# The third differences' product leaves the output bank by a ScalarE copy and an adding DMA of its own

## The chip, the cores and the metric

One core of a Trainium2 chip runs the kernel. The metric is the device time of one execution in microseconds (us). The engines are TensorE (PE in the profile, its weight loads PEld), VectorE (DVE), ScalarE (ACT) and GpSimd (POOL); SyncE (SP) only issues DMAs here.

## The reference

Block-causal attention over 4 x 8 heads, then a soft mixture of 8 experts over all 2304 tokens, then a gated layer. The edit concerns the middle part:

```python
x = attn_out.transpose(0, 2, 1, 3).reshape(B * S, H * D)   # 2304 x 512
logits = x @ w_gate; P = np.exp(logits - logits.max())
for _ in range(8):                                         # balance rows and columns
    P /= P.sum(1, keepdims=True) + 1e-09
    P /= P.sum(0, keepdims=True) + 1e-09
    P *= N / E
for e in range(E):                                         # E = 8, F = 1024, D = 512
    h = np.maximum(x @ w1[e], 0.0)
    out += P[:, e:e + 1] * (h @ w2[e])
...
return silu(out @ w_gate2) * (out @ w_val) @ w_out
```

## The kernel before

The hidden columns of the 8 experts are cut into 16 units of 512 (`NU`), two to an expert. The 2304 tokens stand as two halves of 1152, and a half is cut into five blocks: four of 256 tokens (two tiles of 128) and one of 128. A step (u, b) takes block b of both halves through unit u.

Both matrix products of a step are done as 2 x 2 block products with seven multiplications instead of eight: the operands are X11, X12, X22, the sums S1 and S2, and the differences S3 and S4. Each operand is held as two fp16 parts, and each multiplication is three fp16 matmuls. `products_in` makes the first product (banks `abc` in PSUM, drained at L541 to L561), `sums_out` and `operand` make the operands of the second one (L663 to L693), and `products_out` makes the second product (banks `m_o_b` and `m_o_ac`). TensorE alternates between the two: six matmuls of a `products_in` step, six of a `products_out` step, the latter some steps behind.

In `products_out` the bank `b` of a tile is a running sum: X11, then S2, S3 and X22 are added to it in PSUM, and after each of them `take` carries the half of the result that is then complete out of the bank. So S2's matmuls wait until X11's result has been taken, S3's until S2's, and X22's until S3's. For units 2 to 14 `take` scales a result by the token's routing weight into an SBUF buffer `ev` (from a shared pool, `places`), and a DMA that adds in flight puts it on the accumulator `acc`:

- the first half of the tokens: X11 and S2 fill one buffer, which is added after S2; S4 fills a second one, 512 wide, added after S4;
- the second half: S1's result is copied into the right half of a buffer, S3's result is added to it there by VectorE (L1418), X22's result goes into the left half, and the whole is added after X22.

All other results are taken by ScalarE (L1421). The adds are issued by GpSimd (L1414), one step after the result (`later(1, add)`). The last unit is added to `acc` by VectorE without a buffer.

The same engines do other work in this stage: the weights of the next unit are loaded (L359), reduced (L363), scaled and split (L173, L174) and combined (L292), and the weights of the last layer are converted from a 64-bit raw form (L446 to L458, loaded by L418 into a buffer that is there once). All engines run their instructions in the order of the program, which the Python loop sets.

Of the kernel before, what the change touches and what calls it, by code (L numbers as in the profile page):

```python
# [9 lines left out]
F32 = mybir.dt.float32  # L10
# [3 lines left out]
AF = mybir.ActivationFunctionType  # L14
ALU = mybir.AluOpType
# [9 lines left out]
X11, X12, S4, X22, S1, S2, S3 = range(7)  # L25
# [5 lines left out]
def attention_moe_glu_kernel(  # L31
# [21 lines left out]
    nc = tc.nc  # L53
    B, NPAIR, P, S = qT.shape
    D = 64
    DM = v.shape[2]
    E, _, FF = w1.shape
# [14 lines left out]
    blocks = [(c, min(TB, NH - c)) for c in range(0, NH, TB)]  # L72
# [147 lines left out]
    places = Places(0)  # L220
# [272 lines left out]
    due, load = {}, [0.0]  # L493

    def later(d, f):

        due.setdefault(clock[0] + d, []).append(f)
# [77 lines left out]
    def plain_out(jobs, b, bank, free, every=7, last=False):  # L575


        done = 0
        tiles = tiles_of(b)
        for t, i, ii in tiles:  # L580
            for n, (h, W, evac) in enumerate(jobs):
                p = bank(t * NI + i, n)
                for c in range(2):
                    for j, (r, k, sh, mh) in enumerate(
                        (r, k, sh, mh) for r in range(2) for k in range(2) for sh, mh in ((0, 0), (0, 1), (1, 0))
                    ):
                        nc.tensor.matmul(  # L587
                            p[:, c * TB : (c + 1) * TB],
                            h[t, r][:, sh, k, ii * P : (ii + 1) * P],
                            W[r, c][:, mh, k],  # L590
                            start=c == 0 and j == 0,
                            stop=True,
                            skip_group_check=True,
                        )
                        done += 1
                        if done % every == 0 and not (c == 1 and j == 11):
                            yield True
                if (t, i, ii) == tiles[-1] or (t == 0 and ii == blocks[b][1] // P - 1):
                    places.give(h[t, 0], h[t, 1])
                if last and (t, i, ii) == tiles[-1]:  # L600
                    places.give(*W.values())
                evac(t * NI + i, p)
                free(p)
                if done % every == 0 or n == len(jobs) - 1 and (t, i, ii) == tiles[-1]:
                    yield True
# [642 lines left out]
    with tc.manual_schedule():  # L1248
# [16 lines left out]
        def unweighted(u, dst):  # L1265


            def evac(t, p):
                if u == 0:
                    nc.scalar.activation(dst(t), p, AF.Copy, scale=units[0][2])  # L1270
                else:
                    nc.vector.scalar_tensor_tensor(dst(t), p, units[1][2], dst(t), op0=ALU.mult, op1=ALU.add)

            return evac
# [58 lines left out]
        acc = accp.tile([P, NT, DM], F32, tag="acc", name="acc")  # L1333
# [6 lines left out]
        def m(name):  # L1340
            tag = mfree.popleft()
            t = ps_m1.tile([P, DM], F32, tag=tag, name=f"m_{name}")
            mtag[id(t)] = (tag, t)
            return t
# [32 lines left out]
        def scale_acc():  # L1377

            x = unscaled.popleft()
            nc.scalar.activation(acc[:, x], acc[:, x], AF.Copy, scale=pr[:, x, 0:1])  # L1380

        def expert_out(u, b):
            h = hts.pop((u, b))
            if u < 2:
                f = unweighted(u, lambda t: acc[:, t])
                yield from plain_out([(h, units[u][1], f)], b, lambda t, n: m(f"{u}_{b}_{t}"), mdone, 7, b == NB - 1)
                return
            if b == 0:
                for _ in steps:
                    pass  # L1390
                bg.until((u, 1))
                pe = pes[u] = small.tile([P, NT], F32, tag="pe", name=f"pe_{u}")
                nc.vector.tensor_scalar(pe, pr[:, :, u * FU // FF], units[u][2], None, op0=ALU.mult)

            def take(i, t, cols, ps, what=None):
                if t is None:
                    while u == 2 and (i in unscaled or NI + i in unscaled):
                        scale_acc()
                    return
                x = t * NI + i  # L1400
                p = pes[u][:, x : x + 1]
                a = acc[:, x, cols]
                wide = cols.stop - cols.start > TB
                load[0] += 280 if wide else 165
                if u == NU - 1:
                    nc.vector.scalar_tensor_tensor(a, ps, p, a, op0=ALU.mult, op1=ALU.add)
                    return
                k = (i, t, what == S4)
                if k not in ev:
                    ev[k] = places.take(f"ev{u}_{b}_{x}_{what}", F32)  # L1410
                e = ev[k].rearrange("p a b -> p (a b)")

                def add(x=x, e=e, k=k):
                    nc.gpsimd.dma_start(acc[:, x], e, accum_op=ALU.add)  # L1414
                    places.give(ev.pop(k), left=8)

                if what == S3:
                    nc.vector.scalar_tensor_tensor(e[:, cols], ps, p, e[:, cols], op0=ALU.mult, op1=ALU.add)  # L1418
                else:
                    load[0] -= 280 if wide else 165  # L1420
                    nc.scalar.activation(e[:, cols], ps, AF.Copy, scale=p)  # L1421
                if what in (S2, S4, X22):
                    later(1, add)

            yield from products_out(f"o{u}_{b}", b, h, units[u][1], m, mdone, take, b == NB - 1)

        pes, ev = {}, {}
# [298 lines left out]
```

## Time and profile before

| | |
|---|---|
| median of 3 runs | 2119.81 us (2118.15 to 2122.05) |
| the profiled execution | 2121.61 us, span 2119.8 us |
| TensorE busy in the span | 1968.2 us (93%) |
| VectorE | 1685.4 us (80%) |
| ScalarE | 1335.6 us (63%) |
| GpSimd | 537.0 us (25%) |
| units 2 to 14 leave the banks | from 480 to 1632 us |

Busy time is the sum of the intervals in which an engine executes; the rest is idle, and the trace names for each idle interval what ended it. Matmuls overlap, so the mean time of one is longer than the step from one to the next.

### The profile page before, as it was taken

To read this page: it belongs to the slowest core of one execution; us is meant where nothing else is said; L and a number is where in the kernel's file an instruction comes from. 1 tells how busy PE (TensorE), PEld (TensorE's weight loads), DVE (VectorE), ACT (ScalarE), POOL (GpSimd) and SP (SyncE) were. 2 spreads that over 40 slices of the span, in tenths; PEclk is the share of its full clock that TensorE was granted. 3 is DMA by queue.
4 is the path that set the end of the run, shared out by engine and by line. 5 is a ranking of instruction groups with operands and counts; after the bars stand their busy time and mean duration, and the time that the engine had idled before them with its cause. 6 is when DMAs were issued, how large, how long until landed. Compare 5 with 4: busy or idle time off the path is not lost.

```text
span 2119.8 us, 47322 instructions
## 1 busy us (share of the span) xinstructions
PE 1968.2 (93%) x18378; PEld 1683.5 (79%) x18378; DVE 1685.4 (80%) x3739; ACT 1335.6 (63%) x2823; POOL 537.0 (25%) x808
## 2 busy tenths in 40 slices
PE   6789899799999999999999999999899988999998
PEld 3456676698888888888888888888788877888887
DVE  7887775678888888888888788888887877666766
ACT  5666666348776777767777677777665566543442
POOL 4534444002222222222222222222222132100000
PEclk8889999899999999999999999999999999999999
DMA  5333331315666656766566675666757100201111
GB/s 152 110 99 100 88 108 39 120 31 105 123 163 121 155 111 119 162 127 155 110 122 156 128 160 120 144 131 125 165 120 175 31 16 1 84 23 29 53 41 51
DMA packets 152705, 221.07 MB, mean 104 GB/s; under 512 B 15392, under 2 KB 69664, under 8 KB 152480
## 3 DMA queue, kind: packets, MB, share of 16 engines
q0 software_dynamic: 50544, 92.04, 25.5%
q1 hardware_dynamic: 101936, 126.01, 19.5%
q8 instruction: 144, 2.36, 0.5%
q14 instruction: 81, 0.66, 0.1%
HBM read 90.98 MB, written 24.38 MB: 54 GB/s over the span
## 4 chain that ended last, share of the span: by engine, by line
PE 51%; DVE 21%; issue 4%; ACT 3%; DMA 2%; POOL 0%; SPq 0%; DVEq 0%; ACTq 0%; POOLq 0%
PE abc_m_b L524 10%; PE m_o_b L632 10%; PE m_o_ac L632 7%; PE abc_m_c L524 5%; PE abc_m_a L524 3%; PE m_go_b L632 3%; PE abc_g_b L524 3%; DVE m_t L691 3%; PE abc_v_b L524 3%; DVE m_h L183 2%; PE m_go_ac L632 2%; DVE w L174 2%; DVE m_h L667 2%; PE abc_g_c L524 1%; PE abc_v_c L524 1%
## 5 line engine op out<-in xcount | busy, mean ns | idle before, releaser
L524 PEld LDWEIGHTS <-w 128*128 128x128 f16 x6720 | 614.3, 99 | 126.2 <-issue 58.3
L632 PEld LDWEIGHTS <-m_h 128*128 128x128 f16 x5292 | 516.4, 98 | 84.2 <-issue 20.2
L1414 POOL DMA_DIRECT2D acc<-ev x351 | 302.8, 874 | 945.9 <-ACT ev L1421 758.5
L524 PE MATMUL abc_m_b<-xs,w 128*128 128x256 f16 (+1 forms) x3840 | 483.1, 266 | 38.2 <-DVE m_t L546 33.6
L632 PE MATMUL m_o_b<-w,m_h 128*128 128x256 f16 x3024 | 408.2, 274 | 19.1 <-ACT ev L1421 16.7
L632 PE MATMUL m_o_ac<-w,m_h 128*128 128x256 f16 x2268 | 310.8, 273 | 0.0
L524 PE MATMUL abc_m_c<-xs,w 128*128 128x256 f16 (+1 forms) x1920 | 231.6, 264 | 7.0 <-ACT m_r L760 5.1
L1421 ACT ACTIVATE ev<-m_o_b,pe 128x256 f32<-128x256 f32 x351 | 160.6, 473 | 66.6 <-PE m_o_b L632 60.3
L663 ACT ACTIVATE m_h<-m_t 128x512 f16<-128x512 f32 (+1 forms) x210 | 122.3, 583 | 85.0 <-DVE m_t L561 60.1
L1421 ACT ACTIVATE ev<-m_o_ac,pe 128x256 f32<-128x256 f32 (+1 forms) x234 | 134.3, 578 | 52.4 <-PE m_o_ac L632 51.4
L173 ACT ACTIVATE w<-wr,ws 128x512 f16<-128x512 f32 x210 | 150.0, 719 | 22.7 <-DVE ws L376 19.4
L174 DVE SCALAR_TENSOR_TENSOR w<-wr,ws,w 128x512 f16<-128x512 f32 x210 | 156.4, 746 | 7.6 <-ACT w L173 7.6
L670 ACT CAST m_h<-m_t 128x512 f16<-128x512 f32 (+1 forms) x210 | 121.6, 579 | 50.7 <-DVE m_t L691 49.8
L183 DVE TENSOR_TENSOR m_h<-m_t,m_h 128x512 f16<-128x512 f32 (+1 forms) x210 | 132.9, 634 | 6.1 <-ACT m_h L670 5.8
L667 DVE SCALAR_TENSOR_TENSOR m_h<-m_t,m_h 128x512 f16<-128x512 f32 (+1 forms) x210 | 130.2, 633 | 1.6 <-ACT m_h L663 1.6
L524 PEld LDWEIGHTS <-gg_w 128*128 128x128 f16 x1260 | 113.5, 98 | 20.9 <-issue 9.5
L632 PEld LDWEIGHTS <-g_h 128*128 128x128 f16 x1134 | 111.7, 99 | 19.5 <-issue 5.4
L524 PEld LDWEIGHTS <-gv_w 128*128 128x128 f16 x1260 | 113.6, 98 | 13.2 <-issue 1.7
L983 POOL TENSOR_SCALAR e<-e,r 128x64 f32<-128x64 f32 (+2 forms) x144 | 78.1, 548 | 168.5 <-DVE r L978 106.9
L524 PE MATMUL abc_m_a<-xs,w 128*128 128x256 f16 (+1 forms) x960 | 118.8, 264 | 0.0
L587 PEld LDWEIGHTS <-m_h 128*128 128x128 f16 x864 | 83.7, 99 | 16.9 <-issue 7.0
L363 DVE TENSOR_REDUCE wmx<-wr 128x1 f32<-128x512 f32 x128 | 86.2, 679 | 10.3 <-DMA wr<-in_w_dram 9.9
(315 smaller groups left out, 3310.9 us busy)
## 6 DMA issues: line engine op xcount, KB each, us to landing
acc<-ev POOLq DMA_DIRECT2D x351, 256.0 KB, 3.9
wr<-in_w_dram SPq DMA_DIRECT2D x128, 256.0 KB, 4.9
st<-hl SPq DMA_DIRECT2D x48, 144.0 KB, 3.6
raw_g<-in_w_gate_dram SPq DMA_DIRECT2D x12, 512.0 KB, 4.5
raw_v<-in_w_val_dram SPq DMA_DIRECT2D x12, 512.0 KB, 4.5
raw_o<-in_w_out_dram SPq DMA_DIRECT2D x12, 512.0 KB, 4.9
scr_g<-gg SPq DMA_DIRECT2D x21, 256.0 KB, 3.1
scr_v<-gv SPq DMA_DIRECT2D x21, 256.0 KB, 3.1
```

Of the source, the lines that this page charges most:

```text
L173: nc.scalar.activation(hi, src, AF.Copy, scale=s)
L174: return lambda: nc.vector.scalar_tensor_tensor(lo, src, s, hi, op0=ALU.mult, op1=ALU.subtract)
L183: nc.vector.tensor_sub(lo, src, hi)
L363: nc.vector.tensor_reduce(g["mx"][:, k : k + 1], g["b"][k // 2][k % 2], axis=AX.XY, op=ALU.max, apply_absolute_value=True)
L524: nc.tensor.matmul(ps[:, f], W[o][:, sh, k, f * P : (f + 1) * P], xs[:, o, mh, k, c0 : c0 + n], start=x not in begun, stop=True, skip_grou ...
L587: nc.tensor.matmul(p[:, c * TB : (c + 1) * TB], h[t, r][:, sh, k, ii * P : (ii + 1) * P], W[r, c][:, mh, k], start=c == 0 and j == 0, stop ...
L632: nc.tensor.matmul(ps, h[o][:, sh, k, ii * P : (ii + 1) * P], W[o][:, mh, k], start=o in (X11, X12) and k == 0 and j == 0, stop=True, skip ...
L663: nc.scalar.activation(hi, src, AF.Relu)
L667: nc.vector.scalar_tensor_tensor(lo, src, 0.0, hi, op0=ALU.max, op1=ALU.subtract)
L670: nc.scalar.copy(hi, src)
L1414: nc.gpsimd.dma_start(acc[:, x], e, accum_op=ALU.add)
L1421: nc.scalar.activation(e[:, cols], ps, AF.Copy, scale=p)
```

## The change

For S3, `take` no longer adds into the tile's buffer. ScalarE writes the scaled result into a new buffer that both tiles of the block share, and when the block's last tile is in it, an adding DMA of its own puts it on the right half of the second half's rows of `acc`. The tile's old buffer then holds S1 and X22 only, and is added after X22 as before.

```diff
@@ take, for units 2 to 14 @@
+                if what == S3:
+                    k = (b, S3)
+                    ii, n = i - blocks[b][0] // P, blocks[b][1] // P
+                    if k not in ev:
+                        ev[k] = places.take(f"ev{u}_{b}_s3", F32)
+                    e = ev[k]
+                    nc.scalar.activation(e[:, ii], ps, AF.Copy, scale=p)
+                    load[0] -= 165
+
+                    def add2():
+                        nc.gpsimd.dma_start(acc[:, x - ii : x + 1, cols], e[:, :n], accum_op=ALU.add)
+                        places.give(ev.pop(k), left=8)
+
+                    if ii == n - 1:
+                        later(1, add2)
+                    return
                 k = (i, t, what == S4)
...
-                if what == S3:
-                    nc.vector.scalar_tensor_tensor(e[:, cols], ps, p, e[:, cols], op0=ALU.mult, op1=ALU.add)
-                else:
-                    load[0] -= 280 if wide else 165
-                    nc.scalar.activation(e[:, cols], ps, AF.Copy, scale=p)
+                load[0] -= 280 if wide else 165
+                nc.scalar.activation(e[:, cols], ps, AF.Copy, scale=p)
```

`load` is counted but decides nothing. TensorE's and SyncE's instructions keep their order. On the other engines I show unit 5, block 2 (tiles 4 and 5 of the first half, 13 and 14 of the second), where names are tile_block_row_number. VectorE before:

```order
L667 SCALAR_TENSOR_TENSOR m_3_h_11186<-m_3_t_11153,m_3_h_11186 128x512 [waits Activation_49]
L1418 SCALAR_TENSOR_TENSOR ev_2_13_4_11195<-m_o_2_0_b,pe_10541,ev_2_13_4_11195 128x256 [waits PE_49,Activation_49]
L174 SCALAR_TENSOR_TENSOR w_6_0_11197<-wr_1_00_10938,ws_1_11175,w_6_0_11197 128x512 [waits Activation_49]
L292 TENSOR_TENSOR wr_1_00_10938<-wr_1_01_10940,wr_1_00_10938 128x512 [waits DMASW3_49,DVE_49]
L561 TENSOR_TENSOR m_3_t_11125<-m_3_t_11125,abc_m_3_c 128x512 [waits PE_49]
L1418 SCALAR_TENSOR_TENSOR ev_2_14_4_11214<-m_o_2_1_b,pe_10541,ev_2_14_4_11214 128x256 [waits PE_49,Activation_49]
L174 SCALAR_TENSOR_TENSOR w_6_1_11216<-wr_1_10_10942,ws_1_11175,w_6_1_11216 128x512 [waits DMASW1_49,Activation_49]
```

The two L1418 rows go; the other rows keep their order. ScalarE before, from the first S1 result (`ev_2_13_4`) on:

```order
L1421 ACTIVATE ev_2_13_4_11195<-m_o_2_0_ac,pe_10541 128x256 [waits PE_49]
L173 ACTIVATE w_6_0_11197<-wr_1_00_10938,ws_1_11175 128x512 [waits DMAHW6_49,DVE_49]
L1421 ACTIVATE ev_2_14_4_11214<-m_o_2_1_ac,pe_10541 128x256 [waits PE_49]
L173 ACTIVATE w_6_1_11216<-wr_1_10_10942,ws_1_11175 128x512 [waits DMAHW0_49,DMASW1_49]
L663 ACTIVATE m_3_h_11240<-m_3_t_11205 128x512 [waits DVE_49]
L173 ACTIVATE w_6_2_11249<-wr_1_11_10944,ws_1_11175 128x512 [waits DMAHW1_49,DMASW2_49]
L663 ACTIVATE m_3_h_11259<-m_3_t_11125 128x512 [waits DMASW3_49,DVE_49]
```

and with the change:

```order
L1434 ACTIVATE ev_2_13_4_11229<-m_o_2_0_ac,pe_10571 128x256 [waits DVE_49,PE_49]
L173 ACTIVATE w_6_0_11231<-wr_1_00_10970,ws_1_11209 128x512 [waits DMAHW6_49,DVE_49]
L1434 ACTIVATE ev_2_14_4_11248<-m_o_2_1_ac,pe_10571 128x256 [waits PE_49]
L173 ACTIVATE w_6_1_11250<-wr_1_10_10974,ws_1_11209 128x512 [waits DMAHW0_49,DMASW2_49]
L1414 ACTIVATE ev_2_s_11264<-m_o_2_0_b,pe_10571 128x256 [waits PE_49]
L663 ACTIVATE m_3_h_11275<-m_3_t_11239 128x512 [waits DMASW3_49,DVE_49]
L1414 ACTIVATE ev_2_s_11264<-m_o_2_1_b,pe_10571 128x256 [waits PE_49]
L173 ACTIVATE w_6_2_11284<-wr_1_11_10976,ws_1_11209 128x512 [waits DMAHW1_49,DMASW4_49]
L663 ACTIVATE m_3_h_11294<-m_3_t_11159 128x512 [waits DVE_49]
L1434 ACTIVATE ev_2_4_2_11304<-m_o_2_0_ac,pe_10571 128x512 [waits DMASW5_49,PE_49]
```

Two copies (L1414, both into `ev_2_s`) have come in, each waiting for TensorE, one ahead of each L663. GpSimd before:

```order
L1414 DMA acc<-ev_2_4_0_11089 128x512 [waits DMASW5_49,Activation_49]
L1414 DMA acc<-ev_2_5_0_11098 128x512 [waits DMASW6_49,Activation_49]
L1414 DMA acc<-ev_2_4_2_11268 128x512 [waits DMASW5_49,Activation_49]
L1414 DMA acc<-ev_2_5_2_11286 128x512 [waits DMASW6_49,Activation_49]
L1414 DMA acc<-ev_2_13_4_11195 128x512 [waits DMASW1_49,DVE_49,Activation_49]
L1414 DMA acc<-ev_2_14_4_11214 128x512 [waits DMASW2_49,DVE_49,Activation_49]
```

and with the change:

```order
L1430 DMA acc<-ev_2_4_0_11123 128x512 [waits DMASW6_49,Activation_49]
L1430 DMA acc<-ev_2_5_0_11132 128x512 [waits Activation_49]
L1418 DMA acc<-ev_2_s_11264 128x2x256 [waits Activation_49]
L1430 DMA acc<-ev_2_4_2_11304 128x512 [waits DMASW6_49,Activation_49]
L1430 DMA acc<-ev_2_5_2_11322 128x512 [waits DMASW7_49,DMASW2_49,Activation_49]
L1430 DMA acc<-ev_2_13_4_11229 128x512 [waits DMASW3_49,DMASW0_49,Activation_49]
L1430 DMA acc<-ev_2_14_4_11248 128x512 [waits DMASW4_49,Activation_49]
```

One adding transfer of 128x2x256 has come in ahead of S4's two. The last adds of the second half (`ev_2_13_4`, `ev_2_14_4`) waited for VectorE's addition and now wait for earlier transfers. On TensorE the first X22 matmul of each tile waited for VectorE and now waits for ScalarE.

## Rows read from the trace of the kernel before

**Rows 1.** The page, its first line.

```profile
span 2119.8 us, 47322 instructions
```

**Rows 2.** Stage: us; PE, PEld, DVE, ACT, POOL busy; clock; DMA share, GB/s.

```profile
480.00:1632.00 1152.00, 1096.70 (x10384) 976.43 (x10383) 987.53 (x1963) 823.57 (x1636) 301.86 (x351) 0.99 0.64 137
```

**Rows 3.** TensorE's waits in the stage: us in total, times, longest.

```profile
PE abc_m_b L524 <- DVE m_t L546: 26.7, 17, 2.4
PE m_o_b L632 <- ACT ev L1421: 16.5, 17, 1.9
PE abc_m_c L524 <- ACT m_r L760: 5.1, 5, 1.2
PE abc_m_b L524 <- ACT m_t L549: 2.8, 5, 1.8
```

**Rows 4.** The chain that ended last, in the stage: shares, pieces (start, us, what).

```profile
by line: PE m_o_b L632 17.1%; PE abc_m_b L524 16.6%; PE m_o_ac L632 11.7%; PE abc_m_c L524 7.7%; issue 6.4%; PE abc_m_a L524 4.5%; DVE m_t L691 4.5%; DVE m_h L183 4.0%; DVE w L174 3.3%; DVE m_h L667 2.7%; DVE ev L1418 1.5%; DVE m_r L691 1.5
...
719.10 0.66 PE m_o_b L632 x6
...
1032.06 5.47 DMA raw_v<-in_w_val_dram
1205.45 4.46 DMA raw_v<-in_w_val_dram
```

**Rows 5.** Groups of instructions in the stage: busy us, mean ns, idle before.

```profile
L1418 DVE SCALAR_TENSOR_TENSOR ev<-m_o_b,pe,ev 128x256 f32<-128x256 f32 x117 | 56.2, 481 | 27.4 <-PE m_o_b L632 24.5 <-ACT w L173 2.2
L1421 ACT ACTIVATE ev<-m_o_b,pe 128x256 f32<-128x256 f32 x348 | 159.3, 473 | 65.3 <-PE m_o_b L632 60.3 <-DVE pe L1393 2.9
L1414 POOL DMA_DIRECT2D acc<-ev x351 | 302.8, 874 | 945.9 <-ACT ev L1421 758.5 <-issue 98.5 <-DVE m_r L691 11.5
```

**Rows 6.** Pieces of the same chain, the first and last of eight gaps.

```profile
525.32 0.44 issue
...
1593.52 0.49 issue
1594.02 0.48 DVE ev L1418
```

**Rows 7.** Busy times and timeline before a stall.

```profile
788.80:801.80 13.00, 11.93 (x145) 10.97 (x144) 12.75 (x22) 10.17 (x23) 3.45 (x4) 1.00 0.48 83
...
791.42 0.63 ACT L663 ACTIVATE m_h<-m_t 128x512 f16<-128x512 f32 x1 [1.68 <-DVE m_t L561]
...
799.53 0.62 ACT L670 CAST m_h<-m_t 128x512 f16<-128x512 f32 x1 [1.02 <-DVE m_t L691]
...
801.75 0.83 PE L524 MATMUL abc_m_b<-xs,w 128*128 128x128 f16 x12 [1.07 <-DVE m_t L546]
```

**Rows 8.** Timeline before another stall.

```profile
713.35 0.62 ACT L670 CAST m_h<-m_t 128x512 f16<-128x512 f32 x1 [0.49 <-DVE m_t L691]
...
716.96 0.83 PE L524 MATMUL abc_m_b<-xs,w 128*128 128x128 f16 x12 [2.02 <-DVE m_t L546]
```

**Rows 9.** Queue 0 (packets, MB, share of 16 engines) and its adding transfers.

```profile
q0 software_dynamic: 50544, 92.04, 25.5%
...
acc<-ev POOLq DMA_DIRECT2D x351, 256.0 KB, 3.9
```

**Rows 10.** Timeline around a raw load; ScalarE's waits for such loads.

```profile
768.93 0.82 PE L632 MATMUL m_o_b<-w,m_h 128*128 128x256 f16 x6
...
771.20 0.67 ACT L446 ACTIVATE f_g<-raw_g 128x512 f32<-128x512 f32 x1 [2.25 <-DMA raw_g<-in_w_gate_dram]
...
774.17 0.82 PE L632 MATMUL m_o_b<-w,m_h 128*128 128x256 f16 x6
...
ACT f_v L446 <- DMA raw_v<-in_w_val_dram: 12.8, 3, 5.0
ACT f_g L446 <- DMA raw_g<-in_w_gate_dram: 9.7, 3, 4.8
ACT f_o L446 <- DMA raw_o<-in_w_out_dram: 9.4, 3, 5.1
```

## The prediction

> **What bounds the kernel now.** I read the page's spans first, then the stage in which the edited lines run, then TensorE's waits there, then the chain that ended last, then the timeline around single stalls.
>
> The profiled execution took 2121.6 us, 1.8 us more than its span [rows 1]; it lies 1.8 us above the median of the runs, so a difference found on it is carried to the median as it stands. The edited lines run from 480 to 1632 us. In these 1152 us TensorE is busy for 1096.7, so it stands still for 55.3; VectorE is busy for 987.5 (86%), ScalarE for 823.6 (71%), GpSimd for 301.9 (26%), and the transfer engines for 0.64 [rows 2]. The granted clock there is 0.99, its upper level, so the clock has no part in this.
>
> Nearly all of the standstill has a releaser in the table of waits: 26.7 us for VectorE to take the first sum out of an input bank (L546), 16.5 us for ScalarE's scaled copies out of an output bank (L1421), 5.1 and 2.8 us for two other ScalarE reads [rows 3]. These are 44 short stalls, three or four in each of the 13 units, none over 2.4 us. Between them TensorE runs at its own pace. No saving in this stage can exceed 55 us.
>
> The chain of work shows what makes those stalls. Between TensorE's pieces it runs through long unbroken stretches of VectorE, and the additions that the change removes hold 1.5% of the stage: 17.3 us [rows 4]. So VectorE is behind in bursts, not throughout.
>
> **The change, part by part.**
>
> *The addition leaves VectorE.* There are 117 of them (9 tiles in each of 13 units) at 481 ns, 56.2 us in all [rows 5]. Only what lies on the chain can shorten the run: 17.3 us. VectorE also stood idle for 24.5 us before some of them, until TensorE had finished the third product [rows 5], with other work behind them in the queue; in the chain this shows as gaps before an addition, eight of 0.44 to 0.49 us from 525.32 to 1593.52, 3.7 us together [rows 6]. They go into the lower bound, not into the sum.
>
> *A scaled copy joins ScalarE.* The same form (128x256 from PSUM) takes 473 ns [rows 5]; 117 of them are 55.3 us and bring ScalarE from 71 to 76% of the stage, while VectorE falls to 81%. ScalarE's queue is in order, so what stands behind a copy waits until TensorE has finished the product. I followed two stalls by hand.
>
> Before the one at 801.75 VectorE is busy for 12.75 of 13.0 us and ScalarE for 10.17; ScalarE stands idle for 1.68 us until VectorE's sum and, later, 1.02 us until its next difference; then VectorE reaches L546 late, and TensorE has stood for 1.07 us [rows 7]. Two additions, 0.96 us, leave this stretch. Both idle times are longer than that, so the earlier start passes through to L546: 0.96 us.
>
> Before the stall of 2.02 us at 716.96 ScalarE is nearly packed. It waits only 0.49 us for the difference that its conversion at 713.35 needs [rows 8], and the two copies fall into the same stretch. Of the 0.96 us only some 0.49 arrive.
>
> Together 1.45 of 1.92 us, three quarters. I take this share of the chain's 17.3 us: 13.0 us. The bounds are all of it with the gaps (21.0 us) and nothing (ScalarE packed everywhere).
>
> The Trainium skill, TensorEngine Tiling (Array Packing), section PSUM Bottleneck, advises to use both ScalarE and VectorE for taking results out of PSUM, which speaks against a change that gives the second product's results to ScalarE alone. The trace agrees with it in the packed stretch at 713.35 and not in the one at 801.75; by the rule alone the gain would be nothing, which is the first rival below.
>
> *65 more adding transfers.* Each is issued by GpSimd for 0.87 us [rows 5]; twice the rows per transfer might double that. So 57 to 114 us are added on an engine that is 26% busy and has nothing else to do in this stage; nobody waits for its issuing. By queue 0's share, one adding transfer costs 0.255 x 2119.8 / 351 = 1.54 us of all 16 engines and 144 packets [rows 9]. The new ones carry half rows of two tiles: by bytes 52 x 1.54 + 13 x 0.77 = 90 us, by packets (52 x 272 + 13 x 144 = 16016 against 50544) 171 us. The stage's share goes from 0.64 to between 0.72 and 0.79.
>
> That matters at one place. Five of the chain's longest pieces are loads of raw gate, value and output weights, 4.46 to 5.47 us, 24.4 us together [rows 4]. If they lengthened as the share grows (12 to 23%), that would be 2.9 to 5.6 us; the lower end of the bound is nothing. I take 2 us, since the new transfers start near a block's third difference product, and the raw loads followed in the timeline start before it.
>
> *Waits that are new.* The last add of a tile now waits for the third differences' transfer, because both add to the same half of the tile. It is issued three output steps later (4.0 us: a step is six matmuls of output and six of input, 0.66 us in the chain for either [rows 4]), and an adding transfer lands after 3.9 us in the median [rows 9], so GpSimd stands for a microsecond or so, and behind it in its queue stand only other adds, for whose landing TensorE does not wait in this stage [rows 3]. I take nothing. The X22 matmuls now wait for ScalarE instead of VectorE. Between the third product's end (768.93 + 0.82) and X22's start (774.17) lie 4.4 us [rows 10], of which the copy needs 0.47, so ScalarE may be 3.9 us late at no cost. I take nothing and come back to it as a rival.
>
> *One more buffer* of the shared pool per block is held; it shifts which buffer comes next, TensorE's order is unchanged. Nothing.
>
> Sum: -13.0 + 2.0 = -11.0 us: 2110.6 us for the profiled execution, **2108.8 us** for the median.
>
> **Rivals.**
>
> *ScalarE takes VectorE's place (no change).* What the bursts lose on VectorE they pay on ScalarE. For it: 81% busy of ScalarE before most stalls, and 0.49 us of slack at 713.35. Against it: the idle times of 1.68 and 1.02 us. If a fifth of the chain's share is left, 3.5 us, less the 2 us of transfers: 2118 us. The TensorEngine Tiling section named above leads here.
>
> *The backlog dissolves (faster still).* All of the chain's additions and the gaps before them go, 21.0 us, and the raw loads keep their time: 2098.8 us. For it: with the addition its waits for TensorE leave VectorE too. Against it: VectorE stays at 81%, and in several stretches only one addition lies on the chain.
>
> *ScalarE stuck behind a raw load (slower).* ScalarE's conversion of raw weights stands in its queue until the load has landed, up to 5.1 us [rows 10]. VectorE did not stand in that queue; the new copy does. Where the conversion is ahead of the copy, the copy comes 5.1 + 0.67 + 0.47 us after ScalarE began to wait, 1.8 us more than the 4.4 us of cover; the effect decides once ScalarE reaches the copy over 3.9 us late. With the nine long waits of this kind, 16 us; even with 9 us of the gain kept, 2126 us. In the case at 771.20 the wait was 2.25 us and the copy would still be early by 2 us, which speaks against it.
>
> **How the numbers follow.** Forecast (2104 to 2114 us): 0.48. Backlog dissolves: 0.15. ScalarE takes over: 0.22. Stuck behind the raw load: 0.15. A measurement of this kernel tells 0.2%, 4.2 us, from no change. Faster: the first two and a little of the third, 0.65. Same: most of the third and a little of the last, 0.21. Slower: 0.14. The range from 2098 to 2122 leaves out a third of the second case and nearly all of the last, 2 in 10.
>
> **What would show it.** VectorE's busy time in the stage falls by 56 us and ScalarE's rises by 55; GpSimd has 416 adding transfers of acc instead of 351. TensorE's wait for L546 falls from 26.7 us to under 20, and its standstill in the stage from 55 to about 44. The raw loads on the chain stay below 5.7 us. I am wrong if TensorE's waits for ScalarE grow by as much as those for VectorE shrink, if X22 matmuls show up as waiting for L1414, or if the chain's raw loads lengthen by over a microsecond each.

## The result

The changed kernel takes 2096.55 us (median of 4 runs, 2094.22 to 2098.93); the kernel before, run beside it, takes 2120.72 us. The ratio is 0.9886 (95% interval 0.9869 to 0.9903): 24.2 us, 1.1% faster. That is below the range given (2098 to 2122 us) and 12 us below the number, 2108.8 us. The profiled execution after the change took 2095.47 us.

First the page after the change: span, and busy time by engine.

```profile
span 2093.7 us, 47441 instructions
...
PE 1956.0 (93%) x18378; PEld 1677.2 (80%) x18378; DVE 1640.9 (78%) x3622; ACT 1381.9 (66%) x2940; POOL 613.7 (29%) x873
```

From here on I cut the stage by its own work, from the first scaled copy into `ev` to the last one, so that the same 10401 matmuls lie in it. One row of busy times before (columns as in [rows 2]):

```profile
476.40:1630.70 1154.30, 1098.79 (x10401) 978.07 (x10400) 987.82 (x1970) 825.87 (x1640) 301.02 (x349) 0.99 0.64 136
```

and the same cut after:

```profile
472.40:1603.00 1130.60, 1088.39 (x10401) 972.97 (x10401) 943.68 (x1853) 871.72 (x1758) 376.96 (x414) 1.00 0.74 152
```

The stage is 23.7 us shorter. Behind it nothing moved: 489.1 us are left after the last copy before (2119.8 - 1630.7), 490.7 us after (2093.7 - 1603.0). It also begins 4.0 us earlier; nothing is edited there, and its start lay between 471.7 and 477.4 us in all the profiles of this study, so that is scatter.

The reader is to see two differences in the two rows. TensorE's standstill (length less its busy time) fell from 55.5 to 42.2 us, 13.3 us. And its busy time fell too, from 1098.79 to 1088.39 us, 10.4 us for the same matmuls. That second part is in no term of the prediction.

TensorE's waits after the change, in the stage (columns of [rows 3]):

```profile
PE abc_m_b L524 <- DVE m_t L546: 19.9, 14, 2.4
PE m_o_b L632 <- ACT ev L1434: 10.1, 11, 1.7
PE abc_m_c L524 <- ACT m_r L760: 5.2, 6, 2.0
PE abc_m_b L524 <- ACT m_t L549: 2.9, 5, 1.8
```

VectorE's L546 is waited for less (26.7 us in [rows 3]), and so is ScalarE (L1421 there, 16.5 us, is L1434 here), though ScalarE got the copies. L1414, the new copy, is not in the list. Who waited for it, by that line's own view:

```profile
L1414 ACT ACTIVATE ev_s<-m_o_b,pe x117: 449/474/498, 481.6 to 1599.5; 128x256 f32<-128x256 f32 x117
...
who waited for it (us, times):
  POOL acc L1418: 229.6, 62
```

Only GpSimd, which issues the transfer, waits for it. ScalarE's own waits for the raw weights (last three lines of [rows 10]) have become:

```profile
ACT f_v L446 <- DMA raw_v<-in_w_val_dram: 8.3, 3, 3.3
ACT f_o L446 <- DMA raw_o<-in_w_out_dram: 8.1, 3, 3.6
ACT f_g L446 <- DMA raw_g<-in_w_gate_dram: 7.1, 3, 3.2
```

The chain that ended last, in the stage (columns of [rows 4]):

```profile
by line: PE abc_m_b L524 19.0%; PE m_o_b L632 18.6%; PE m_o_ac L632 13.5%; PE abc_m_c L524 9.0%; issue 5.2%; PE abc_m_a L524 4.8%; DMA wr<-in_w_dram 2.7%; DVE m_t L691 2.4%; DVE m_h L183 2.3%; DVE m_h L667 1.6%; ACT ev L1434 1.6%; DVE w L17
...
597.51 6.01 DMA wr<-in_w_dram
...
1373.31 10.96 DMA wr<-in_w_dram
...
1537.18 4.42 DMA raw_o<-in_w_out_dram
```

TensorE's lines hold more of the chain than in [rows 4], VectorE's less (`m_t` of L691 4.5 to 2.4%, `m_h` of L183 4.0 to 2.3%). The raw loads on it are no longer than before (4.42 us is the longest of four); loads of the next unit's weights (`wr`), none of them among the long pieces before, now are. In one place a new transfer itself lies on it:

```profile
916.57 3.84 DMA acc<-ev_s
```

VectorE's waits for those weight loads, before, after, and in experiment 4, which has no new transfers:

```profile
DVE wmx L363 <- DMA wr<-in_w_dram: 6.0, 8, 1.1
...
DVE wmx L363 <- DMA wr<-in_w_dram: 10.4, 8, 2.0
...
DVE wmx L363 <- DMA wr<-in_w_dram: 6.3, 7, 1.5
```

The new transfers and the groups that issue them (columns of [rows 5]; in the last two lines size and median time to landing):

```profile
L1430 POOL DMA_DIRECT2D acc<-ev x349 | 303.5, 898 | 607.5 <-ACT ev L1434 399.1 <-issue 99.2 <-ACT m_t L549 28.1
...
L1418 POOL DMA_DIRECT2D acc<-ev_s x65 | 73.6, 1132 | 236.3 <-ACT ev_s L1414 229.6 <-DMA acc<-ev 6.6
...
acc<-ev POOLq DMA_DIRECT2D x351, 256.0 KB, 4.3
...
acc<-ev_s POOLq DMA_DIRECT2D x52, 256.0 KB, 4.3
```

**Where the second part came from.** I cut the stage into windows of 2 us, read the granted clock of each, and added up 2 us x (1 - clock). Before, this gives 11.9 us, in seven separate places, each of which loses some 1.7 us; after, 1.7 us, in one place. Take these off TensorE's busy time and the same work is left in both: 1098.79 - 11.9 = 1086.9 and 1088.39 - 1.7 = 1086.7 us (in the experiments below, but for the seventh, which adds matmuls, this remainder lies between 1084.0 and 1089.0 us, so the reading is good to a few microseconds). One such place before, in windows:

```profile
1154.00:1156.00 2.00, 0.78 (x12) 0.77 (x12) 1.97 (x5) 1.30 (x3) 0.00 (x0) 0.93 0.00 0
1156.00:1158.00 2.00, 2.00 (x13) 1.40 (x11) 2.00 (x6) 1.22 (x4) 0.00 (x0) 0.50 0.04 8
1158.00:1160.00 2.00, 2.00 (x15) 1.57 (x14) 1.97 (x6) 1.07 (x3) 0.86 (x1) 0.72 0.06 10
```

and in the timeline of TensorE (start, duration, idle time before):

```profile
1155.22 1.02 PE L524 MATMUL abc_m_b<-xs,w 128*128 128x128 f16 x12 [2.37 <-DVE m_t L546]
1156.04 1.48 PE L632 MATMUL m_o_b<-w,m_h 128*128 128x256 f16 x6
...
1160.17 0.82 PE L632 MATMUL m_o_ac<-w,m_h 128*128 128x256 f16 x6
```

TensorE has stood for 2.37 us until VectorE's L546; then the granted clock is 0.50, the 1.2 GHz level, and six matmuls take 1.48 us instead of 0.82. The stage's mean of 0.99 hides it. The same place after the change:

```profile
1139.70 0.83 PE L524 MATMUL abc_m_b<-xs,w 128*128 128x128 f16 x12 [2.37 <-DVE m_t L546]
1140.37 0.82 PE L632 MATMUL m_o_b<-w,m_h 128*128 128x256 f16 x6
```

The standstill is the same, 2.37 us, and this time the clock stays at its upper level. So a standstill of this length goes ahead of a fall, but not each is followed by one. Of the seven falls before, four came behind a single standstill of 2.03 to 2.37 us and three behind two standstills close together (0.99 and 0.85 us, 1.80 and 0.47, 1.21 and 0.85). Single standstills of 2.0 us or more number eight before, four of them followed by a fall, and three after, one of them followed by a fall.

What one fall costs can be read from a second profile of the changed kernel (experiment 10), in which the clock did fall at this place. The next long standstill, first in the profile above, then the same two places in the second profile:

```profile
1207.27 0.38 PE L632 MATMUL m_o_b<-w,m_h 128*128 128x256 f16 x2 [1.43 <-ACT ev L1434]
...
1143.48 0.83 PE L524 MATMUL abc_m_b<-xs,w 128*128 128x128 f16 x12 [2.37 <-DVE m_t L546]
1144.14 1.41 PE L632 MATMUL m_o_b<-w,m_h 128*128 128x256 f16 x6
...
1212.67 0.38 PE L632 MATMUL m_o_b<-w,m_h 128*128 128x256 f16 x2 [1.43 <-ACT ev L1434]
```

From the one standstill's end to the other's it is 67.57 us without the fall and 69.19 us with it. So 1.6 of the 1.7 us had not been caught up there, and the standstill at the end is as long as before. The mean granted clock of whole executions is 0.977 over 39 runs of the kernel before and 0.981 over 8 of the changed one; 0.0037 x 2100 us is 8 us, so the profiled pair, with 10.2 us, shows a little more of this than the average.

### The profile page after: what moved, and what is told of

Its sections match the earlier page's. It is cut to its first block, busy times and chain, and to the rows that moved or that the text cites. A ratio compares the mean times of both kernels' runs of the same rounds, so it can differ in the third digit from the quotient of the medians.

```text
span 2093.7 us, 47441 instructions
## 1 busy us (share of the span) xinstructions
PE 1956.0 (93%) x18378; PEld 1677.2 (80%) x18378; DVE 1640.9 (78%) x3622; ACT 1381.9 (66%) x2940; POOL 613.7 (29%) x873
## 4 chain that ended last, share of the span: by engine, by line
PE 55%; DVE 15%; ACT 5%; issue 3%; DMA 3%; POOL 0%; SPq 0%; ACTq 0%; DVEq 0%; POOLq 0%
PE abc_m_b L524 11%; PE m_o_b L632 11%; PE m_o_ac L632 8%; PE abc_m_c L524 5%; PE abc_m_a L524 3%; PE abc_v_b L524 3%; PE abc_g_b L524 3%; PE m_go_b L632 3%; PE m_go_ac L632 2%; DMA wr<-in_w_dram 2%; DVE m_t L691 2%; PE abc_v_c L524 1%; PE abc_g_c L524 1%; DVE m_h L183 1%; PE m L587 1%
## 5 line engine op out<-in xcount | busy, mean ns | idle before, releaser
L524 PE MATMUL abc_m_b<-xs,w 128*128 128x256 f16 (+1 forms) x3840 | 478.6, 265 | 31.8 <-DVE m_t L546 26.7
L632 PE MATMUL m_o_b<-w,m_h 128*128 128x256 f16 x3024 | 404.9, 273 | 11.5 <-ACT ev L1434 10.1
L1434 ACT ACTIVATE ev<-m_o_b,pe 128x256 f32<-128x256 f32 x351 | 161.8, 475 | 80.9 <-PE m_o_b L632 73.6
L174 DVE SCALAR_TENSOR_TENSOR w<-wr,ws,w 128x512 f16<-128x512 f32 x210 | 156.6, 747 | 10.2 <-ACT w L173 10.1
L1434 ACT ACTIVATE ev<-m_o_ac,pe 128x256 f32<-128x256 f32 (+1 forms) x234 | 134.7, 580 | 44.4 <-PE m_o_ac L632 42.0
L663 ACT ACTIVATE m_h<-m_t 128x512 f16<-128x512 f32 (+1 forms) x210 | 122.7, 584 | 49.1 <-DVE m_t L561 29.1
L1418 POOL DMA_DIRECT2D acc<-ev_s x65 | 73.6, 1132 | 236.3 <-ACT ev_s L1414 229.6
L183 DVE TENSOR_TENSOR m_h<-m_t,m_h 128x512 f16<-128x512 f32 (+1 forms) x210 | 133.0, 635 | 12.2 <-ACT m_h L670 11.5
L524 PEld LDWEIGHTS <-gg_w 128*128 128x128 f16 x1260 | 113.6, 98 | 20.9 <-issue 9.4
```

Source lines behind the costliest of these rows:

```text
L174: return lambda: nc.vector.scalar_tensor_tensor(lo, src, s, hi, op0=ALU.mult, op1=ALU.subtract)
L183: nc.vector.tensor_sub(lo, src, hi)
L524: nc.tensor.matmul(ps[:, f], W[o][:, sh, k, f * P : (f + 1) * P], xs[:, o, mh, k, c0 : c0 + n], start=x not in begun, stop=True, skip_grou ...
L632: nc.tensor.matmul(ps, h[o][:, sh, k, ii * P : (ii + 1) * P], W[o][:, mh, k], start=o in (X11, X12) and k == 0 and j == 0, stop=True, skip ...
L663: nc.scalar.activation(hi, src, AF.Relu)
```

## The experiments

Theory: VectorE's 117 additions alone made the bursts in which L546 is late; without them TensorE stands still for less, and because fewer of the standstills are long, its clock falls less often. Rivals: the gain comes from the new buffer and the transfer of its own (X22's add no longer waits for S3's); or the clock difference is chance. The kernel before was run beside each group of kernels: 2119.14 us (the first four, 19 runs), 2121.04 (the next four, 13 runs), 2120.38 (the last two, 7 runs). Edits are on the changed kernel unless said otherwise; standstill and time lost at the lower clock level are worked out as above.

**1. The changed kernel with S3's product written by VectorE.**

```diff
-                    nc.scalar.activation(e[:, ii], ps, AF.Copy, scale=p)
+                    nc.vector.tensor_scalar_mul(e[:, ii], ps, p)
```

> The changed kernel, but VectorE writes the third product's scaled result into the shared buffer instead of ScalarE; the adding transfer of its own stays. Theory 1 (VectorE's time): the gain comes from the 56 us of additions, and the 24 us of waiting before them, that leave VectorE. Then nearly all of it is lost again: 2113 to 2122 us, TensorE's wait for L546 back near 27 us, and low-clock stretches in the stage back to about seven. Rival (buffers and waits): the gain comes from the separate buffer and transfer, by which the tile's last add no longer waits for an addition. Then it stays near 2097 us.

Measured: 2121.39 us, ratio 1.0008 (0.9995 to 1.002). Stage, group and wait:

```profile
471.70:1625.90 1154.20, 1096.58 (x10401) 976.04 (x10401) 987.33 (x1970) 825.72 (x1640) 377.80 (x414) 0.99 0.73 149
...
L1414 DVE TENSOR_SCALAR ev_s<-m_o_b,pe 128x256 f32<-128x256 f32 x117 | 56.1, 479 | 25.0 <-PE m_o_b L632 24.3
...
PE abc_m_b L524 <- DVE m_t L546: 27.4, 17, 2.6
```

Buffer and transfers are those of the changed kernel, VectorE's time is that of before, and the time and the L546 wait are those of before: standstill 57.6 us, 8.6 us lost at the lower level in 5 places. The buffer and the transfer path do not bring the gain.

**2. The changed kernel with one extra operation of VectorE at each place.** Nobody reads its result. It reads constants and the token's routing weight and waits for nothing of TensorE's.

```diff
+                    nc.vector.scalar_tensor_tensor(extra, wide_ones, p, wide_ones, op0=ALU.mult, op1=ALU.add)
```

> The changed kernel, and VectorE does one more instruction of the removed form's size (128x256, from constants into a scratch tile) at each place of the removed addition; it waits for nothing and nobody waits for it. Theory 1: VectorE's busy time alone brings most of the loss back; without the waits for TensorE about two thirds: 2108 to 2118 us. If the waits for TensorE ahead of the addition were what mattered, it stays below 2103 us. Rival (buffers and waits): 2097 us.

Measured: 2117.43 us, ratio 0.9994 (0.9984 to 1.0005).

```profile
472.40:1624.50 1152.10, 1099.26 (x10401) 977.91 (x10401) 986.62 (x1970) 873.54 (x1757) 376.24 (x414) 0.99 0.73 149
...
L1416 DVE SCALAR_TENSOR_TENSOR extra<-ones,pe 128x256 f16<-128x256 f32 x117 | 55.9, 478 | 0.0
...
PE abc_m_b L524 <- DVE m_t L546: 25.8, 19, 2.4
```

ScalarE still has the copies, nothing waits for the extra operation's result, and it never stood waiting itself (0.0 behind the bar). Yet all but 1.7 us of the gain are lost (2119.14 - 2117.43; interval -1.1 to 3.4), with a standstill of 52.8 us and 11.9 us lost at the lower level in 7 places. So most of the gain is VectorE's bare time. Experiment 1, in which the operation also waits for TensorE, is 4.0 us slower than this one (ten runs each), although ScalarE is spared the copies there; so the additions' waits for TensorE are worth about that much or a little more.

**3. The third product's result not taken out of the bank at all, and 4. copied but not transferred.** Its matmuls stay in both; the output lacks the third product.

```diff
                 if what == S3:
+                    return
```

```diff
                     def add2():
-                        nc.gpsimd.dma_start(acc[:, x - ii : x + 1, cols], e[:, :n], accum_op=ALU.add)
```

> The changed kernel without anything that takes the third product's result out of the bank for units 2 to 14: no copy, no buffer, no transfer, so the output lacks that term. It shows what the 117 copies and 65 transfers still cost. Theory 1, with my estimate of 25% given back by ScalarE and 2 us by the transfers: 2088 to 2094 us. If ScalarE and the transfers give back nothing: within 2 us of the changed kernel, 2095 to 2099 us.

> The changed kernel with the copies and the buffer, but without the 65 adding transfers, so the output lacks the third product. By my term for the transfers: 2 us faster than the changed kernel, and the raw loads on the chain shorter by 0.4 to 0.8 us each. If the transfers are hidden: no difference that can be told (under 2 us either way).

Measured: 2090.62 us, ratio 0.9862 (0.9842 to 0.9881), without copies and transfers; 2092.3 us, 0.9869 (0.9851 to 0.9887), with the copies. The stage of the first:

```profile
473.60:1599.70 1126.10, 1089.11 (x10403) 974.59 (x10402) 943.11 (x1853) 826.68 (x1641) 301.09 (x349) 1.00 0.65 139
```

and of the second:

```profile
473.20:1598.50 1125.30, 1086.76 (x10402) 972.56 (x10401) 943.56 (x1853) 871.11 (x1757) 301.05 (x349) 1.00 0.65 140
```

Standstill is 37.0 and 38.5 us. So VectorE's additions cost 18.5 us of it (55.5 - 37.0), the copies take back 1.5, and the transfers (42.2 in the changed kernel) 3.7. By the medians the copies cost 1.7 us and the transfers 2.7 to 4.5 (a gain of 26.8 us without them, against 24.2 in the result and 22.3 in experiment 10); these intervals overlap. The standstill is the better witness, though it is read from one profile of each; the changed kernel's second profile repeats its own within 0.2 us (42.4, experiment 10).

**5. The change in even units only** (7 of 13, 63 of 117 copies).

```diff
-                if what == S3:
+                if what == S3 and u % 2 == 0:
```

with the old addition kept for the odd ones.

> The change in the even units 2 to 14 only (7 of 13 units); the odd units add the third product on VectorE as before. Theory 1 (VectorE's time): the saving follows the share, 7/13 of 24 us = 13 us: 2104 to 2110 us, and the standstill falls in the even units' stretches and not in the odd ones'. If the gain hangs on one place or on all units together (a threshold of the backlog): near 2097 or near 2119 us.

Measured: 2102.67 us (2100.94 to 2108.2), ratio 0.9921 (0.9905 to 0.9937): 18.4 us, more than expected, and the interval (13.4 to 20.1 us) stays just above a proportional share, 24.2 x 63/117 = 13.0. The profiled run, the slowest of the four, has this stage:

```profile
473.40:1616.60 1143.20, 1094.90 (x10401) 976.32 (x10401) 964.22 (x1907) 850.20 (x1703) 341.20 (x384) 0.99 0.69 144
```

Standstill is 48.3 us: 7.2 of 13.3 us gained, the share of the units. I cut the stage into 13 stretches of equally many matmuls, one for each unit. In the seven even ones standstill is 33.2 us before, 24.1 us here and 24.4 us in the changed kernel; in the six odd ones it is 22.3, 24.2 and 17.8 us. So it fell where the additions had gone, as far as in the changed kernel, and nowhere else. The surplus in time is not explained; where the clock falls differs from run to run.

**6. The changed kernel with the weights' combining (L292) on GpSimd, and 8. the same edit on the kernel before.** If VectorE's time is the limit, taking 108 us more off it (83 us for the experts' weights, 25 us for the last layer's) should help again.

```diff
-            nc.vector.tensor_sub(o, x, y)
+            nc.gpsimd.tensor_tensor(o, x, y, op=ALU.subtract)
```

> The changed kernel, and the differences of the weight blocks (the 128x512 subtractions that take VectorE 694 ns each, 120 of them for the experts) are made by GpSimd. Theory 1: another 80 us leave VectorE in the same stage, so TensorE's standstill there falls from 42 us further, to 20 to 32 us: 2075 to 2090 us. Rival: after the change VectorE is no longer the limit, ScalarE and the loads are; then 2093 to 2100 us, or slower, if GpSimd's longer subtractions hold up the weights and its adds.

> The kernel before (the third product added by VectorE), and the differences of the weight blocks made by GpSimd. Theory 1: any 56 us and more taken from VectorE in this stage do what the change did: 2090 to 2102 us. Rival (the gain hangs on the third product's path): 2115 to 2125 us.

Measured: 2164.89 us, ratio 1.0214 (1.0197 to 1.0231), and on the kernel before 2169.22 us, 1.0231 (1.0216 to 1.0246). Both expectations were wrong. The groups in experiment 6, and its timeline of VectorE and GpSimd at one place:

```profile
L174 DVE SCALAR_TENSOR_TENSOR w<-wr,ws,w 128x512 f16<-128x512 f32 x210 | 201.2, 962 | 15.8 <-ACT w L173 15.8
L292 POOL TENSOR_TENSOR wr<-wr,wr 128x512 f32<-128x512 f32 x120 | 186.8, 1557 | 96.4 <-DVE w L174 55.2 <-ACT m_t L549 22.0 <-PE abc_m_c L524 11.2
...
566.30 4.00 DVE L174 SCALAR_TENSOR_TENSOR w<-wr,ws,w 128x512 f16<-128x512 f32 x3 [0.29 <-ACT w L173]
...
566.15 2.94 POOL L292 TENSOR_TENSOR wr<-wr,wr 128x512 f32<-128x512 f32 x2 [2.50 <-DVE w L174]
...
574.03 0.74 DVE L174 SCALAR_TENSOR_TENSOR w<-wr,ws,w 128x512 f16<-128x512 f32 x1
```

Three of VectorE's L174 take 4.00 us while GpSimd subtracts, 1.33 us each; alone one takes 0.74. VectorE's busy time in the stage became 999 us, more than the 943.7 it had with the subtractions. Standstill rose to 87 us and the time lost at the lower clock level to 18.8 us in 10 places (20.5 us in 11 for experiment 8). The edit did not take work off VectorE's time, so it says nothing against the theory; it repeats its other half, that more standstill comes with more time at 1.2 GHz.

**7. The kernel before with TensorE's idle time filled:** 24 matmuls of 128 columns into a spare bank, their results unused, ahead of X22 in the short block (the 128-token one) of 13 units in the stage.

```diff
+            if o == X22 and n < TB and name[0] == "m" and name[1] != "0" and filler[0]:
+                fill_t = filler[0](f"fill_{name}")
+                for j in range(FILL):
+                    nc.tensor.matmul(fill_t[:, :P], ...)
```

> The kernel before, and TensorE does 24 extra matmuls of 128 columns (about 1.3 us) into a spare bank in front of the X22 matmuls of each unit's short block, where it stands for 1.1 to 2.4 us for VectorE's L546. Their results are not used. If the clock falls because TensorE stands still, the fall after these stalls goes and the others stay: low stretches in the stage from seven to three or fewer, and 2110 to 2116 us. If the clock's falls have nothing to do with these stalls: seven low stretches, and 2119 to 2123 us.

Measured: 2121.11 us, ratio 0.9993 (0.9981 to 1.0006). The time is a miss; the mechanism is as expected.

```profile
472.80:1621.90 1149.10, 1107.77 (x10714) 991.38 (x10714) 987.46 (x1970) 824.30 (x1641) 301.04 (x349) 1.00 0.64 137
...
L525 PE MATMUL m_fill_m<-xs,w 128*128 128x128 f16 x312 | 19.5, 219 | 0.0
...
PE abc_m_b L533 <- DVE m_t L555: 10.3, 13, 1.0
```

VectorE's work is unchanged (987.46 us), the longest wait for the input bank (L555 here) is now 1.0 us instead of 2.4, and the places at the lower clock level fall from 7 to 2, 11.9 to 3.4 us. The mean clock over 10 runs is 0.982 against 0.977. Standstill falls by 14.2 us (55.5 to 41.3), but the filler itself takes about 17 (12 matmuls of 128 columns follow each other in 0.66 us, so 312 take 17.2), and of the balance, 14.2 + 8.5 - 17.2 = 5.5 us in the profile, the median over ten runs shows nothing (the profiled run, 2115.75 us, is the second fastest of the ten); why is open. What it shows is the link: with VectorE's work untouched, fewer long standstills go with fewer falls of the clock. That fewer falls make this kernel faster it does not show.

**9. The changed kernel without weight preparation in the short blocks, and 10. the changed kernel again beside it.** L546's waits lie near the short blocks, and VectorE is filled there by the next unit's weights.

```diff
+                short[0] = u > 1 and b == NB - 1
...
-            background()
+            if not short[0]:
+                background()
```

> The changed kernel, and the preparation of weights takes no step while a unit's short block (128 tokens) goes through the first product; the steps left out are made up in the next block. After the change TensorE's largest standstill is still the wait for L546 in front of the short block's X22, 1.4 to 2.4 us in most units, behind VectorE's work on weights. If VectorE's burst there is what is left, most of that wait goes: the standstill in the stage falls from 42 to 25 to 34 us and the time to 2080 to 2090 us. If the burst only moves into the next block, 2093 to 2100 us.

> The changed kernel once more, beside the run above on the same chip: 2094 to 2099 us, with TensorE standing still for about 42 us in the stage and no more than three low-clock stretches there.

Measured: 2098.01 us, ratio 0.9885 (0.9859 to 0.9912), and 2098.08 us, 0.9894 (0.9869 to 0.9919): no better version. TensorE's waits in experiment 9:

```profile
PE m_o_b L632 <- ACT ev L1434: 20.9, 17, 1.8
...
PE m_w L110 <- DVE w_d L103: 6.3, 7, 1.7
...
PE abc_m_b L524 <- DVE m_t L546: 1.3, 1, 1.3
```

L546 is down to 1.3 us, and the work that was held back makes others late: ScalarE's copies (10.1 to 20.9 us) and the spreading of the weights' maxima over the partitions (L103). Standstill is 46.6 us. The burst moved. The stage of experiment 10:

```profile
474.80:1608.30 1133.50, 1091.10 (x10402) 974.55 (x10401) 943.84 (x1853) 871.16 (x1757) 376.29 (x414) 1.00 0.74 152
```

Its standstill is 42.4 us, and 5.2 us are lost at the lower level in 3 places, so of the two parts of the gain the first repeats closely and the second varies.

## Why the prediction was wrong in size

The sign was right, and so was the mechanism of the term that decides it: VectorE's time. The range was too high, because a second mechanism, the clock, was ruled out. By its own steps:

- **"The granted clock there is 0.99, its upper level, so the clock has no part in this."** This step failed, and with it "No saving in this stage can exceed 55 us" lost its basis, since TensorE's busy time could shrink too. The mean of 1152 us hid seven places at the 1.2 GHz level, 11.9 us together. The changed kernel's profile has 1.7 us left (5.2 in its second profile). By TensorE's busy time this is 7 to 10 us of the 24.2, and most of the 13 us by which the sum missed. Experiments 1, 2 and 7 show the link with the standstills, and the two profiles of the changed kernel show one fall costing 1.6 us; that the falls' number alone sets the time is not shown (experiment 7). Why a given standstill of 2.4 us is or isn't followed by a fall is not settled.
- **"17.3 us [of the chain]"** as the additions' whole weight was good: 18.5 us of standstill went when they were left out with nothing in their place (experiment 3). That most of it is VectorE's own time is shown by experiment 2, which brings back 22.5 us (24.2 - 1.7) of the 28.5 us that experiment 3 gains (10.6 of 18.5 us by standstill). The 17.3 us stood for that bare time alone, so by standstill the match is in part luck.
- **"They go into the lower bound, not into the sum"**, said of the 3.7 us of gaps ahead of the additions, put at nothing what the runs price at 4.0 us or a little more (experiment 1 against 2). This step failed too, at a small size.
- **"Together 1.45 of 1.92 us, three quarters"** was mis-sized. The copies took 4.3 us of the 17.3 in the prediction; they took 1.5 us on the chip (experiments 3 and 4). Two stalls followed by hand did not stand for 44: ScalarE has more slack than the packed one shows.
- **"I take 2 us"** for the transfers' load was too little: 3.7 us by standstill. The transfer share went to 0.74, inside the 0.72 to 0.79 given. But it was not the raw loads that paid on the chain; those landed in 4.9, 4.9 and 5.7 us in the median instead of 4.5, 4.5 and 4.9, and ScalarE waited less for them. The chain has weight loads of 6 to 11 us instead, and VectorE's wait for them is 10.4 us with the new transfers (11.9 us in the second profile) against 6.0 us before and 6.3 us without them, a difference of about that size. Whether the load on the transfer engines does it or the buffer that each of them holds, which the prediction put at nothing, was not separated.
- So the net of the standstill, 13.3 us against 11.0, came near, by three errors that partly cancel (18.5 - 1.5 - 3.7 against 17.3 - 4.3 - 2.0).
- **What would show it:** GpSimd has its 351 + 65 adding transfers; L546's wait fell under 20 us (19.9); the standstill fell to 42.2 (about 44 was named); the raw loads on the chain are at most 4.42 us (under 5.7). VectorE's busy time was to fall by 56 us and ScalarE's to rise by 55; they changed by 44.1 and 45.9. Records of successive VectorE instructions overlap, so 117 x 481 ns overstates the time: experiment 2's 117 extra ones, 55.9 us by themselves, raised busy time by 42.9 us, 367 ns each.

**The rivals.** ScalarE did not take VectorE's place: its waits at the output bank fell from 16.5 to 10.1 us. The Trainium skill, TensorEngine Tiling (Array Packing), section PSUM Bottleneck, advises to use both ScalarE and VectorE for taking results out of PSUM, which led to that rival. Experiment 1, which takes the second product's results with both, is 24.8 us slower than the changed kernel's median, so here the measurement decides against it. ScalarE stuck behind a raw load did not come about: X22 waited for L1414 not once (that rival's own sum, 2119.8 + 16 - 9, gives 2126.8 us and not 2126). "The backlog dissolves" named 21.0 us, close to the total. Its gaps of 3.7 us came about (4.0 us or a little more, experiment 1 against 2), but it had neither the 5.2 us of standstill that copies and transfers take back nor the clock, so that its number comes near is in part luck.

## What to carry to other kernels

A mean clock of 0.99 over a long stage is not the upper level throughout: cut it into short windows, count the places at 1.2 GHz, and look at what stands ahead of them. Where they follow standstills, work taken off the engine that is late in bursts can pay twice, once in the standstill and once in the clock. Busy shares did not tell which engine could take the work (ScalarE, then busy for 77% of the stage, was no obstacle; GpSimd, at 33%, was): ask whether the receiver slows the engine that is to be relieved.

## What the runs showed of the hardware

- The granted clock went to 0.50 in seven places of the stage, each time at a loss of 1.7 us: four times behind a standstill of 2.03 to 2.37 us, three times behind two shorter ones close together (sums of 1.84 to 2.27 us). The Trainium skill, TensorE: Matmul & The Clock Gate, section "A second HAM failure mode: psum-queue depth-cycling", tells of a clock that swings between its levels because TensorE idles briefly between groups of matmuls. The seven places of the kernel before agree with it; the 2.37 us at 1139.70 without a fall show that it is not so each time.
- A subtraction of 128x512 from SBUF on GpSimd (1557 ns; 694 ns on VectorE) lengthens VectorE's operations that run beside it: L174 from 746 to 962 ns in the mean, from 0.74 to 1.33 us where both ran together. The Trainium skill, SBUF — State Buffer, section "Who interferes with whom", states that a VectorE instruction with two inputs in SBUF contends with a GpSimd instruction that reads SBUF; the trace agrees.
- Issuing an adding transfer of two tiles (256 rows of 1 KB) takes GpSimd 1.20 us in the median, of one tile (128 rows of 2 KB, the same bytes) 0.86 us; the 13 transfers of 128 rows of 1 KB also take 0.86 us, so the rows set the difference and not the bytes. (The mean of 1132 ns above is over both kinds of the new ones.) Both 256 KB kinds land after 4.3 us in the median.
